# Holding the fourth batch's DMA transposes until half of the last q has landed, and planning with overlapping VectorE and ScalarE instructions

## The chip, the cores and the metric

One core of one Trainium2 chip. The metric is the device time of one execution in microseconds (us). A "span" is the time from the first to the last instruction on the core; it is about 2 us shorter than the device time.

## The reference, cut to what matters

Four batches of eight heads, 768 tokens, 64 columns a head. Attention is local (16 keys on each side) plus one summary key and value per block of 32. Its output feeds eight experts, weighted by a matrix that eight Sinkhorn iterations balance.

```python
def _attn_ref(q, k, v):                     # (4, 8, 768, 64)
    k_sum = k.reshape(B, H, nb, 32, D).max(axis=3)
    v_sum = v.reshape(B, H, nb, 32, D).mean(axis=3)
    # scores with the near keys (masked band) and with the summaries (+ log 32), one softmax over both
    ...
def _moe_ref(x, w_gate, w1, w2):            # x (3072, 512), 8 experts, F = 1024
    P = np.exp(logits - logits.max())
    for _ in range(8):
        P /= P.sum(1, keepdims=True) + 1e-09
        P /= P.sum(0, keepdims=True) + 1e-09
        P *= N / E
    for e in range(E):
        out += P[:, e:e + 1] * (np.maximum(x @ w1[e], 0.0) @ w2[e])
```

## The kernel before

The kernel does not list its instructions in the order in which they are emitted. It describes units of work (engine, estimated cost in us, what they depend on, a priority), and a planner on the host simulates them once and emits the units in the order of that simulation. On the chip each engine then runs its own fixed order and waits where a semaphore isn't set.

```python
class Plan:
    HOP = 0.15
    ...
    def order(self):
        ...
            for u in left:
                t0 = ready(u)
                for e, cost in u.eng.items():
                    t = max([t0, free.get(e, 0.0)]
                            + [d.end + d.lag + (self.HOP if d.on != e else 0.0) for d in u.deps])
                    best.setdefault(e, []).append((t, u, cost))
            ...
            u.start, u.end, u.on = t, end, e
            free[e] = end            # the engine is free when its unit ends
```

A pair of heads is a chain of such units. Pairs 12 to 15 are the fourth batch; their q and k are transposed by DMAs from SyncE's queue, those of the pairs before by TensorE.

```python
# pair_start, pair_whole: the units of one pair, with their planned costs
U["tr", i, z] = add("SP", 1.4, lambda z=z: tr_dma(i, z), [U["kq"[z], i], U.get(("S", i - 3, 1))] + ...)
U["ks", i] = add("DVE", 0.95, lambda: key_max(i), [U["kT", i, 0], ...])
U["km", i] = add("DVE", 0.23, lambda: key_max_split(i), [U["ks", i]] + ...)
U["Vs", i] = add("DVE", 0.28 if i < PB else 0.7, lambda: block_out(i), [U["vs", i], sc], ...)
U["mk", i, h] = add("DVE", 0.56, lambda h=h: masks(i, h), ...)            # twice
U["ed", i] = add("DVE", 0.78, lambda: edges(i), ...)
U["ss", i, 0] = U["ss", i, 1] = add("PE", 0.22, lambda: summaries_2(i), [U["km", i], U["kT", i, 1], ...])
U["sx", i, h] = add("ACT", 0.46, lambda h=h: summary_exp(i, h), [U["ss", i, h]], ...)
U["no", i, h] = add("DVE", 0.75, lambda h=h: normalize(i, h), ...)        # twice
...
rows = add("DVE", 1.65, sink_rows, prev, 0)                               # 8 routing iterations

def edges(i):                      # four small instructions on 32 partitions each
    for j in range(2):
        q0 = 64 + 32 * j           # where the output starts: partition 64, then 96
        nc.vector.tensor_tensor(out=ee[q0:q0 + 32, ...], in0=er[0:32, ...], in1=band[0:32, ...], op=ALU.mult)
        nc.vector.tensor_tensor(out=ee[q0:q0 + 32, ...], in0=er[96:128, ...], in1=band[96:128, ...], op=ALU.mult)
```

TensorE has plenty of work that no pair needs at once (the first expert's products `hps` and `yps` of earlier batches), and the planner fills with it.

The softmax here doesn't subtract the row's maximum and nothing guards it: scores larger than these inputs give would overflow.

## Time and profile before

| | before |
|---|---|
| time, median of 3 runs | 666.03 us (665.86 to 666.69) |
| span of the profiled run | 664.1 us |
| TensorE busy | 656.6 us, 99% |
| VectorE, ScalarE busy | 550.1 us (83%), 410.9 us (62%) |
| TensorE's idle waits after the first 20 us | one, 0.6 us |

What pair 12 does in the kernel before, on VectorE and TensorE (all engines' timeline, start us, length us):

```profile
91.82 0.95 DVE L335 TENSOR_REDUCE ks<-kT 128x24 bf16<-128x768 bf16 x1
...
92.80 0.22 DVE L341 TENSOR_TENSOR ksT<-ks,own 128x64 bf16<-128x64 bf16 x1
...
94.90 0.49 PE L461 MATMUL ss<-qT,ksT 128*128 128x384 bf16 x2
```

The maximum over each block of keys, its split over the two heads, and the scores with the summaries.

### The profile page before, as it was taken

The numbers are of one execution on the slowest core, as the hardware profiler recorded it, in microseconds if no ns is written. First come the engines' busy times: TensorE is split into PE (matmuls) and PEld (weight loads), VectorE is DVE, ScalarE is ACT, GpSimd is POOL, SyncE is SP. The second block draws the span as 40 slices with busy tenths as digits, with TensorE's granted clock in tenths as the row PEclk, the third lists the DMA queues.
The fourth block names the chain that finished last, engine by engine and source line by source line (L and its number), as shares of the span: only waits on it lengthen the run. The fifth ranks groups of instructions, "written<-read, shape, count | busy, mean of one in ns | idle before, by whom it ended". The sixth has DMA issues, their size and how long they took to land.

```text
span 664.1 us, 13257 instructions
## 1 busy us (share of the span) xinstructions
PE 656.6 (99%) x5131; PEld 435.9 (66%) x5132; DVE 550.1 (83%) x1036; ACT 410.9 (62%) x769; POOL 199.0 (30%) x257
## 2 busy tenths in 40 slices
PE   8999999999999999999999999999999999999997
PEld 4666666545766666666666666666666666666666
DVE  7899897799988887887779877988778877988776
ACT  6677676556885566556665665555655656556652
POOL 8899522100132222212322222223122213222123
PEclk9999999999999999999999999999999999999999
DMA  9999932700953747373754665373838465335656
GB/s 167 181 145 145 143 70 43 128 1 2 157 96 65 126 75 118 64 128 65 110 97 71 121 91 101 64 127 65 127 64 135 73 96 96 64 64 112 157 134 202
DMA packets 112558, 67.89 MB, mean 102 GB/s; under 512 B 77936, under 2 KB 90480, under 8 KB 112496
## 3 DMA queue, kind: packets, MB, share of 16 engines
q0 software_dynamic: 94816, 57.46, 64.9%
q1 hardware_dynamic: 17152, 9.58, 5.9%
q8 instruction: 40, 0.66, 0.4%
q14 instruction: 22, 0.18, 0.1%
q10 hardware_dynamic: 528, 0.02, 0.0%
HBM read 52.45 MB, written 6.29 MB: 88 GB/s over the span
## 4 chain that ended last, share of the span: by engine, by line
PE 96%; DVE 3%; DMA 1%; issue 0%; ACT 0%; POOLq 0%; DVEq 0%
PE yps L815 22%; PE pA L764 22%; PE pY L815 17%; PE pQ L764 11%; PE hps L211 6%; PE yps L216 6%; PE pR L764 5%; PE sg L347 1%; DMA qst<-in_q_dram 1%; PE av L512 1%; PE vs L357 1%; PE tkq L303 1%; PE av L435 1%; DVE xs L543 1%; PE ss L461 1%; PE av L441 1%
## 5 line engine op out<-in xcount | busy, mean ns | idle before, releaser
L815 PEld LDWEIGHTS <-h 128*128 128x128 f16 x2352 | 230.1, 98 | 88.5 <-issue 1.0
L843 POOL DMA_DIRECT2D out_acc<-y x120 | 101.7, 891 | 372.1 <-ACT y L839 110.3
L839 ACT ACTIVATE y<-pY,P_sb 128x256 f32<-128x256 f32 x168 | 79.8, 477 | 123.3 <-PE pY L815 121.6
L830 DVE SCALAR_TENSOR_TENSOR out_acc<-yps,P_sb,out_acc 128x512 f32<-128x512 f32 x128 | 95.1, 744 | 29.0 <-PE yps L815 29.0
L798 DVE TENSOR_TENSOR h<-h 128x1024 f16<-128x1024 f16 x168 | 109.3, 683 | 1.4
L815 PE MATMUL pY<-w,h 128*128 128x256 f16 x672 | 100.0, 273 | 0.6 <-ACT y L839 0.6
L815 PE MATMUL yps<-w2sum,h 128*128 128x256 f16 x672 | 98.4, 273 | 0.0
L764 PE MATMUL pA<-xT,w 128*128 128x512 f16 x336 | 98.3, 379 | 0.0
L815 PE MATMUL yps<-w,h 128*128 128x256 f16 x672 | 93.3, 273 | 0.0
L830 DVE SCALAR_TENSOR_TENSOR out_acc<-pY,P_sb,out_acc 128x512 f32<-128x512 f32 x84 | 62.8, 748 | 29.1 <-PE pY L815 27.4
L764 PEld LDWEIGHTS <-w 128*128 128x128 f16 x672 | 65.8, 98 | 31.6 <-issue 0.2
L764 PEld LDWEIGHTS <-w1sum 128*128 128x128 f16 x504 | 49.3, 98 | 45.0
L786 DVE CUSTOM_DVE_ANT_0 h<-pQ,snap 128x512 f16<-128x512 f32 x84 | 57.6, 685 | 7.0 <-ACT snap L207 4.3
L786 DVE CUSTOM_DVE_ANT_0 h<-pA,snap 128x512 f16<-128x512 f32 x84 | 57.3, 682 | 4.8 <-PE pA L764 4.8
L202 ACT ACTIVATE h<-pA 128x512 f16<-128x512 f32 x84 | 50.6, 603 | 12.6 <-PE pA L764 12.4
L202 ACT ACTIVATE h<-pR 128x512 f16<-128x512 f32 x84 | 50.1, 596 | 8.0 <-PE pR L764 7.7
L207 ACT COPY pR<-pA 128x512 f32<-128x512 f32 x83 | 47.5, 572 | 7.7 <-PE pA L764 6.9
L815 PE MATMUL pY<-w2sum,h 128*128 128x256 f16 x336 | 50.4, 273 | 0.0
L764 PE MATMUL pA<-xsum,w 128*128 128x512 f16 x168 | 50.0, 379 | 0.0
L764 PE MATMUL pR<-xT,w 128*128 128x512 f16 x168 | 50.0, 379 | 0.0
L764 PE MATMUL pQ<-xsum,w1sum 128*128 128x512 f16 x168 | 50.0, 379 | 0.0
L764 PE MATMUL pA<-xsum,w1sum 128*128 128x512 f16 x168 | 50.0, 379 | 0.0
(150 smaller groups left out, 854.3 us busy)
## 6 DMA issues: line engine op xcount, KB each, us to landing
out_acc<-y POOLq DMA_DIRECT2D x120, 256.0 KB, 3.4
w<-in_moe_w_dram POOLq DMA_DIRECT2D x14, 1024.0 KB, 10.7
out_dram<-out_acc SPq DMA_DIRECT2D x24, 256.0 KB, 2.4
qst<-in_q_dram POOLq DMA_DIRECT2D x32, 96.0 KB, 5.3
vx<-in_v_dram POOLq DMA_DIRECT2D x15, 192.0 KB, 6.2
kst<-in_k_dram POOLq DMA_DIRECT2D x24, 96.0 KB, 5.6
w<-in_moe_w_dram POOLq DMA_DIRECT2D x4, 256.0 KB, 7.6
w<-in_moe_w_dram POOLq DMA_DIRECT2D x2, 512.0 KB, 7.7
```

The source lines that it names most:

```text
L202: nc.scalar.activation(out=out, in_=in_, func=AF.Relu, bias=0.0, scale=1.0)
L207: (nc.scalar.copy if eng == "ACT" else nc.vector.tensor_copy)(out=out, in_=in_)
L211: nc.tensor.matmul(hp[:, 0:n], lhsT=w1s[e][:, dk, f * 128:(f + 1) * 128], rhs=xT[:, dk, t0:t0 + n], start=(dk == 0), stop=(dk == KD - 1))
L216: nc.tensor.matmul(yp[:, d], lhsT=h[:, f, c * 128:(c + 1) * 128], rhs=w2s[e][:, f, d], start=(f == 0), stop=(f == KF - 1))
L303: nc.tensor.transpose(t[:, g * 128:(g + 1) * 128], st[:, g, :, :].rearrange("p j d -> p (j d)"), ident)
L764: nc.tensor.matmul(dst[:], lhsT=lhsT, rhs=rhs, start=first and k == 0, stop=k == HK - 1, skip_group_check=True)
L786: nc.vector._custom_dve(dve_ops.TENSOR_ADD_SAT, out=ring(e, p, q)[:, q % 2, blk, :], in0=at[src, e, p, q][:], in1=at.pop(("snap", n, e, p, ...
L798: nc.vector.tensor_tensor(out=h[:, :, out_, :], in0=h[:, :, a, :], in1=h[:, :, b, :], op=op)
L815: nc.tensor.matmul(dst[:, d], lhsT=lhsT, rhs=rhs, start=f == 0 and n in (1, 5, 2), stop=f == HF - 1, skip_group_check=True)
L830: nc.vector.scalar_tensor_tensor(out=o, in0=y, scalar=scalar, in1=o, op0=ALU.mult, op1=ALU.add)
L839: nc.scalar.activation(out=at[key][:, d], in_=src, func=AF.Copy, bias=0.0, scale=P_sb[:, t, e:e + 1])
L843: nc.gpsimd.dma_start(out=o, in_=at.pop(("y", e, p, c, key))[:], accum_op=ALU.add)
```

## The change

It has two intents. The transposes of pair 12, and behind them in SyncE's queue all eight of the batch, are not to mix with the last loads; so GpSimd copies one column of the last q into the targets of pair 12's transposes, which then have to wait for it. And the planner is to know that a VectorE or ScalarE instruction can start before the one ahead has quite ended: after every unit its engine is taken to be free 0.07 or 0.09 us before the unit's end. The routing rows are planned at 1.5 us, not 1.65.

```diff
 class Plan:
     HOP = 0.15
+    OVERLAP = {"DVE": 0.07, "ACT": 0.09}
...
-            free[e] = end
+            free[e] = end - self.OVERLAP.get(e, 0.0)
...
-    X_BY_DMA = 12
-    WHOLE = 10
+    X_BY_DMA = {12, 13, 14}
+    WHOLE = {10, 11, 12, 13, 14, 15}
...
+        def loads_landed(i):
+            st = at["st", NP - 1, 1]
+            for t in (kT[i % NB][0:32, 0:1], qT[i % NB][0:32, W:W + 1]):
+                nc.gpsimd.tensor_copy(out=t, in_=st[0:32, 0, 0, 0:1])
...
             if i >= BY_DMA:
+                hold = U.get(("tr", i - 1, 1))
+                if i == BY_DMA:
+                    hold = add("POOL", 0.3, lambda: loads_landed(i), [last[0], U["q", NP - 1]] + war_k + war_q, prio)
+                    last[0] = hold
                 for z in range(2):
                     U["tr", i, z] = add("SP", 1.4, lambda z=z: tr_dma(i, z),
-                                        [U["kq"[z], i], U.get(("S", i - 3, 1))] + (war_k, war_q)[z], prio)
+                                        [U["kq"[z], i], U.get(("S", i - 3, 1)), hold] + (war_k, war_q)[z], prio)
...
-            load_pair(i, "" if i == PB else "kqv")
+            for n in range(i, NP) if i == BY_DMA else [i] if PB < i < BY_DMA else []:
+                load_pair(n, "kqv")
...
-            rows = add("DVE", 1.65, sink_rows, prev, 0)
+            rows = add("DVE", 1.5, sink_rows, prev, 0)
```

(Left out: the places where a comparison with 10 or 12 becomes a test of membership, with the same members.)

More of the change, by code (lines that the diff above doesn't have):

```diff
@@ L384, in scores @@
             dst = [[sg[:, j, :] for j in range(2)], None]
-            if i >= WHOLE:
+            if i in WHOLE:
                 dst[1] = at["sg", i, 1] = [bank("a", "sg1") for _ in range(2)]
-            score_mms(i, dst, range(G if i >= WHOLE else HG))
+            score_mms(i, dst, range(G if i in WHOLE else HG))
         def scores_1(i):
@@ L948, in pair_whole @@
             deps = [U["kT", i, 0], U["kT", i, 1], U.get(("ed", i - 2))]
-            bufs = [Buffer("s")] + (2 * [None] if i < WHOLE else [Buffer("a"), Buffer("a")])
-            U["S", i, 0] = U["S", i, 1] = add("PE", 0.4 if i < WHOLE else 0.6, lambda: scores(i), deps, prio,
+            bufs = [Buffer("s")] + (2 * [None] if i not in WHOLE else [Buffer("a"), Buffer("a")])
+            U["S", i, 0] = U["S", i, 1] = add("PE", 0.4 if i not in WHOLE else 0.6, lambda: scores(i), deps, prio,
                                               opens=[x for x in bufs if x is not None])
             U["X", i, 0] = add("ACT", 0.97, lambda: score_exp(i, 0), [U["S", i, 0]], prio, uses=bufs[:1])
-            if i < WHOLE:
+            if i not in WHOLE:
                 buf = Buffer("s")
@@ L978, in pair_whole @@
                                     [U["A", i, h], U.get(("x", i - 2))], prio, uses=[buf])
-            if i >= X_BY_DMA and i % PB < PB - 1:
+            if i in X_BY_DMA:
                 U["xt", i] = add("SP", 1.5, lambda: x_dma(i), [U["no", i, 0], U["no", i, 1]], prio)
@@ L1100, in transposed @@
             nc.gpsimd.tensor_copy(out=warm[:, 1:2], in_=qT[r][0:32, W:W + 1])
-            if X_BY_DMA < NP:
+            if NP - 2 in X_BY_DMA:
                 nc.gpsimd.tensor_copy(out=warm[:, 4:5], in_=xT[0:32, PB - 2, (B - 1) * S:(B - 1) * S + 1])
@@ L1108 @@
         last[0] = add("POOL", 0.3, transposed, [last[0], U["near", NP - 1]] + [U["kT", NP - 1, z] for z in range(2)]
-                      + [U["x", i] for i in range(X_BY_DMA, NP - 1)])
+                      + [U["x", i] for i in X_BY_DMA])
         load("w1n", lambda: load_w1(1), 0.85, 5.0)
```

## The prediction

> **What bounds the kernel now.** I read the page's head first, then the chain of work that ended last, TensorE's waits after the start, and only then the stretch that the change touches (60 to 120 us), engine by engine. The page:
>
> ```profile
> span 664.1 us, 13257 instructions
> PE 656.6 (99%) x5131; PEld 435.9 (66%) x5132; DVE 550.1 (83%) x1036; ACT 410.9 (62%) x769; POOL 199.0 (30%) x257
> ...
> PE 96%; DVE 3%; DMA 1%; issue 0%; ACT 0%; POOLq 0%; DVEq 0%
> ```
>
> The reader is to see that TensorE is nearly the whole chain, and that all else on it is 4% of 664.1, some 27 us. A busy TensorE need not be at its rate, so I checked that in the groups of TensorE for 200 to 600 us (names, shape, count, busy us, mean ns):
>
> ```profile
> L815 PE MATMUL pY<-w,h 128*128 128x256 f16 x525 | 78.9, 273 | 0.0
> L764 PE MATMUL pA<-xT,w 128*128 128x512 f16 x264 | 77.7, 379 | 0.0
> ...
> L764 PE MATMUL pQ<-xT,w1sum 128*128 128x512 f16 x132 | 39.3, 379 | 0.0
> ```
>
> All groups of that answer together are 1840 matmuls of 256 columns and 924 of 512. The means, 273 and 379 ns, are latencies: in the chain eight of the first start within 0.87 us (109 ns each) and four of the second within 0.86 us (215 ns each). 1840 x 0.109 + 924 x 0.215 = 200.6 + 198.7 = 399 us of 400. So the 400 us have no hole to win. TensorE's waits from 20 us to the end are a single line:
>
> ```profile
> PE pY L815 <- ACT y L839: 0.6, 1, 0.6
> ```
>
> That one wait is at 657.5 us, in the last tile. In the first 20 us the waits are 1.3 us (zeros), 0.8 us (first q) and 0.3 us (k), all before 7 us. What the schedule could still win is thus about 0.6 us at the end and small switches in the first 30 us.
>
> Now the transposes on SyncE's queue, the scores on TensorE that use them, and GpSimd's loads (start us, length us):
>
> ```profile
> 66.23 1.32 SPq L330 DMA_TRANSPOSE kT<-kst  x1
> 68.01 1.56 SPq L330 DMA_TRANSPOSE qT<-qst  x1
> ...
> 78.48 2.25 SPq L330 DMA_TRANSPOSE kT<-kst  x1
> ...
> 87.99 1.21 SPq L330 DMA_TRANSPOSE qT<-qst  x1
> ```
> ```profile
> 91.06 0.59 PE L347 MATMUL sg<-qT,kT 64*128 64x160 bf16 x12
> ...
> 97.72 0.59 PE L347 MATMUL sg<-qT,kT 64*128 64x160 bf16 x12
> ...
> 103.58 0.59 PE L347 MATMUL sg<-qT,kT 64*128 64x160 bf16 x12
> ...
> 109.26 0.59 PE L347 MATMUL sg<-qT,kT 64*128 64x160 bf16 x12
> ```
> ```profile
> 75.52 0.82 POOL L284 DMA_DIRECT2D qst<-in_q_dram  x1 [0.75 <-DMA kst<-in_k_dram]
> 76.62 1.02 POOL L289 DMA_DIRECT2D vx<-in_v_dram  x1 [0.28 <-DMA qst<-in_q_dram]
> 87.93 0.57 POOL L377 DMA_DIRECT2D Ve<-vx  x1 [10.29 <-PE av L441]
> ```
>
> The last four score groups are pairs 12 to 15 (16 pairs, the fourth batch last). Pair 12's first transpose is issued at 66.23, its scores run at 91.06: 25 us early. The last load of q is issued at 75.52, and GpSimd then idles for 10.29 us.
>
> **What the Trainium skill says.** "DMA: Bandwidth & Descriptors", section "Issuing engines are not separate DMA queues": transfers from all queues end on the same 16 engines and interleave. The trace agrees: the load of half a q takes 5.3 us to land (median of 13) between 40 and 66 us, without transposes, and 7.7 us (of 5) between 66 and 80 us, after the first two. The same page, "Rules for kernel authors", says that a transpose next to ordinary DMAs needs nothing: so the new wait isn't needed for correctness, it only moves traffic; no run here shows more. "Perfetto Trace Analysis", section "Identifying the Most-Contended Engine", calls matmul busy time a bad measure of distance to the roofline; the 273 ns against 109 ns above agree, hence the count of starts. "VectorE: DVE Perf Modes", section "The DRAIN you can't avoid", says that the next operation doesn't start until the pipe is empty. By the trace's recorded ends the starts do overlap: two add-relu of 0.68 us start 0.60 us apart (138.99 and 139.59), while subtractions that read the one before start 0.72 us apart (134.28 and 135.00). The change's 0.07 us fits the first kind.
>
> **The change part by part.**
> 1. The sets for which pairs go by DMA or score whole are written differently, with the same members: 0.
> 2. Loads of pairs 12 to 15 become one block. GpSimd issues them back to back already, one pair in about 4.3 us (k's first halves at 63.07, 67.41, 71.65), in the same order: 0 on the path.
> 3. A new GpSimd step of two tiny copies from the last q into the targets of pair 12's transposes. Similar copies there took 0.17 and 0.21 us: 0.4 us, in the idle 10.29 us. Off the path.
> 4. That step holds SyncE's transposes. Without transposes in flight GpSimd's waits of 0.42 + 0.75 us before the last two q halves (73.95 and 75.52) should go, so the last half is issued near 74.3; plus 5.5 us to land, 79.8; plus copies and semaphores, 80.3. Estimate: pair 12's transposes start 14 us later, near 80.3. On quiet engines one was issued 1.39 us after another (84.48 to 85.87) and landed in 2.7 us. Eight take 11.1 us: the last is issued near 90.0, landed near 93. Both operands of pair 12 have landed by 80.3 + 1.4 + 2.7 = 84.4, or 6.7 us before its scores at 91.06; pair 13 by 87.2 (10.5 us before 97.72); pair 14 by 90.0 (13.6); pair 15 by 92.8 (16.5). A key maximum on VectorE (0.95 us) and its split (0.22 us) fit before the summaries at 94.90. So the whole delay is hidden. Removed: two or three us of slower landing for loads that nobody on the path waits for: 0.
> 5. The planner's overlap (0.07 us VectorE, 0.09 us ScalarE) and 1.5 for 1.65 us alter only the order in which instructions are emitted. No instruction gets shorter and the count of matmuls stays. The real step from one row half of the routing iteration to the next instruction is 1.53 us (124.58 to 126.11), so the new figure is closer. Worth between -0.8 us (the wait of 0.6 at the end and some head switches) and +1 us (a new bubble where VectorE is later than planned); centre -0.2.
> Sum: 666.03 - 0.2 = 665.8 us.
>
> **Rivals.** (a) The hold becomes the path: pair 12's scores wait. For: fixed orders do not wait politely. Against: 6.7 us of slack, and first-layer matmuls of earlier batches fill TensorE there. If the last q lands 10 us late, up to 3 us are lost: 669. (b) VectorE binds in the routing stretch, 121 to 164 us, where it is busy 8.7 to 9.6 of each 10 us. An overlap that dependent steps do not have puts its results later than planned and TensorE waits. Against: TensorE is 100% busy there, a multiply-add that needs the routing result first runs at 169.26, 5 us after it is done at 163.98. Would make 667 to 668. (c) Transposes without rival traffic let the fourth batch and the routing end several us sooner: still nothing, since TensorE has other work throughout; 665.8. (d) The better plan repairs the end and the head: 664.9.
>
> **Range and chances.** (c) changes nothing, (d) takes 0.9, small bubbles of (b) add 1: 8 in 10 between 664.8 and 667.0. Faster by 2% would need 13.3 us, more than all of TensorE's idle time (664.1 - 656.6 = 7.5 us): 0.01. Slower by 2% needs a stall of 13 us, twice pair 12's slack: 0.02. Within 2%: 0.97.
>
> **What would show it.** Right: first transpose near 80 us, the eight steadily about 1.4 us apart, loads of the fourth batch landing in about 5.5 us instead of 7.7; pair 12's scores without a wait for a DMA; TensorE's busy time within 0.5 us of 656.6 and no waits between 20 and 655 us. Wrong: a TensorE wait ended by kT, qT or their DMA near 80 to 110 us (a), or waits ended by VectorE after 121 us (b), or a much changed wait in the first 30 us or the last 6 us (d). A longer span with the same waits would mean a lower granted clock, not this change.

## More of the kernel before

On the page, each digit is the busy share, in tenths, of one fortieth of the span (16.6 us):

```profile
DVE  7899897799988887887779877988778877988776
```

VectorE is the second engine: in the first seven slices, where attention runs, it is busy for 70 to 100% of the time. So a result can come late by standing far back in VectorE's queue.

## The result

| | before | after |
|---|---|---|
| time, median (6 runs each) | 666.25 us (665.86 to 666.69) | 666.88 us (666.82 to 668.52) |
| ratio | | 1.0014, 95% interval 1.0001 to 1.0027 |
| span of the profiled run | 664.1 us | 665.3 us |

A ratio is the mean time of one kernel's runs over that of the other's in the same rounds, so not quite the ratio of the medians. All outputs are right. The change costs 0.6 us by the medians: within 2%, inside the predicted range, and in the other direction than the predicted centre. The times alone show it barely: the interval starts at 1.0001, and that of a second set of runs (after_again, below) is 0.9992 to 1.0018, though both pairs of medians differ by 0.63 us. What carries it is the traces.

The page of the changed kernel:

```profile
span 665.3 us, 13288 instructions
...
PE 657.8 (99%) x5131; PEld 435.9 (66%) x5132; DVE 562.9 (85%) x1051; ACT 403.7 (61%) x754; POOL 199.4 (30%) x259
```

TensorE has the same 5131 matmuls, and 1.2 us more of "busy". (Fifteen instructions went from ScalarE to VectorE, so the planner changed more than the order. That is not what costs the time: true_costs, below, has 1052 on VectorE, 562.4 us busy, and takes the time of the kernel before.) Its waits after 20 us are again a single line, the old one:

```profile
PE pY L822 <- ACT y L846: 0.6, 1, 0.6
```

So by the usual views nothing has happened, and the span is still 1.2 us longer. The hold did what it was meant to do (GpSimd's and SyncE's timelines):

```profile
75.86 0.82 POOL L285 DMA_DIRECT2D qst<-in_q_dram  x1 [0.42 <-issue]
...
80.52 0.18 POOL L338 COPY kT<-qst 32x1 bf16<-32x1 bf16 x1 [2.82 <-ACT out_acc L208]
```
```profile
80.73 1.32 SPq L331 DMA_TRANSPOSE kT<-kst  x1
...
91.19 1.21 SPq L331 DMA_TRANSPOSE qT<-qst  x1
```

The first transpose goes at 80.73 instead of 66.23, the eighth at 91.19, 1.4 to 2.1 us apart; all have landed by 93.92. The routing's first matmul ran at 121.62 (before 123.62) and its last at 156.54 (before 163.09): 6.5 us sooner, for no gain. It is the overlap's order that brings it forward and not the hold: the last one ran at 156.12 without the hold (overlap_only, below) and at 164.97 with the hold but without the overlap (hold_sink).

**Where the time went.** The ends of matmuls are modelled, and a wait of some 0.2 us can vanish inside the modelled tail of the group ahead. It shows only in starts. TensorE's timeline of the changed kernel:

```profile
84.74 0.50 PE L557 MATMUL tx<-ident_x,xs 128*128 128x128 f16 x6
85.07 0.50 PE L364 MATMUL vs<-vx,m_blk 128*128 128x128 bf16 x6
...
89.72 0.50 PE L557 MATMUL tx<-ident_x,xs 128*128 128x128 f16 x6
90.28 0.50 PE L468 MATMUL ss<-qT,ksT 128*128 128x384 bf16 x2
```

The same six transposes of 128 columns, both "0.50 us" long. After the first the next group starts 0.33 us later, after the second 0.56 us later: a wait of 0.23 us for `ksT` that no waits view shows. I did this for the whole trace: for each two consecutive TensorE instructions the step from start to start, less the median step of such a couple (told by the two shapes) over the traced kernels; what is over 0.04 us I call a **short wait**, and I sum those that are not inside one group of the same kind. (The 0.6 us wait of the waits view is one of them, 0.73 us by this measure.)

| short waits, us | before | after |
|---|---|---|
| 20 to 125 us | 0.57 (at 20.6, 43.7, 66.2) | 1.49 (at 20.9, 33.8, 49.4, 53.7, 55.9, 71.6, 72.7, 90.3, 108.9) |
| 125 to 640 us | 0.00 | 0.09 |
| 640 us to the end | 1.02 | 0.90 |

1.49 + 0.09 + 0.90 - 0.57 - 1.02 = 0.89 us. The span without the head (from TensorE's first transpose of q on) grew from 657.10 to 657.93 us, 0.83 us. So these waits are the loss. The other 0.37 us of the 1.2 are in that head, whose loads vary from run to run: a second trace of the changed kernel had 6.87 us there where the first had 7.33, and the same short waits within 0.02 us at the same places.

Why was `ksT` late? VectorE's timeline of the changed kernel:

```profile
84.45 0.55 DVE L419 TENSOR_TENSOR em<-er,band 128x768 bf16<-128x768 bf16 x1
85.02 0.19 DVE L427 TENSOR_TENSOR Ee<-er,band 32x80 bf16<-32x80 bf16 x1
85.22 0.20 DVE L431 TENSOR_TENSOR Ee<-er,band 32x80 bf16<-32x80 bf16 x1
85.43 0.19 DVE L427 TENSOR_TENSOR Ee<-er,band 32x80 bf16<-32x80 bf16 x1
85.63 0.20 DVE L431 TENSOR_TENSOR Ee<-er,band 32x80 bf16<-32x80 bf16 x1
85.86 0.29 DVE L370 TENSOR_TENSOR Ve<-vs,own_n 64x128 bf16<-64x128 f32 x1
...
86.59 0.54 DVE L205 TENSOR_SCALAR h<-hps 128x384 f16<-128x384 f32 x1
87.06 0.94 DVE L342 TENSOR_REDUCE ks<-kT 128x24 bf16<-128x768 bf16 x1
87.92 0.18 DVE L549 RECIPROCAL rc<-av 128x6 f32<-128x6 f32 x1
...
90.02 0.21 DVE L348 TENSOR_TENSOR ksT<-ks,own 128x64 bf16<-128x64 bf16 x1
```

Pair 12's key maximum is done at 88.0, but its split `ksT` stands behind two normalizations and another block copy, and VectorE does these without a gap until 90.02. The transposes are not the reason: that k had landed at 83.6. And the reader sees which instructions overlap: the relu at 86.59 lasts 0.54 us and the next starts 0.47 us after it; the four edge products last 0.19 or 0.20 us and start 0.20 to 0.21 us apart, and the first starts 0.57 us after a mask of 0.55 us. They do not overlap at all.

The Trainium skill, "VectorE: DVE Perf Modes", section "Two Vector instructions with no wait between them", gives a model for it: an instruction is held until all before it have finished when one of its inputs or its output starts in another group of 32 partitions than the last one in the same memory did. The edges read from partition 0 and 96 in turn and write to 64 and 96, so all four should be held; the trace agrees.

Summed for one pair (eight VectorE units: key maximum, split, block copy, two masks, edges, two normalizations): the old plan has 0.95 + 0.23 + 0.70 + 2 x 0.56 + 0.78 + 2 x 0.75 = 5.28 us, the new one 8 x 0.07 less, 4.72 us. The trace's steps give 0.86 + 0.13 + 0.73 + 0.47 + 0.57 + 0.84 + 0.68 + 0.70 = 4.98 us. The old plan was 6% too slow, the new one is 5% too fast.

### The profile page after: what moved, and what is told of

Read it like the earlier page. It is cut to its first block, busy times and chain, and to the rows that moved or that the text cites. A ratio compares the mean times of both kernels' runs of the same rounds, so it can differ in the third digit from the quotient of the medians.

```text
span 665.3 us, 13288 instructions
## 1 busy us (share of the span) xinstructions
PE 657.8 (99%) x5131; PEld 435.9 (66%) x5132; DVE 562.9 (85%) x1051; ACT 403.7 (61%) x754; POOL 199.4 (30%) x259
## 4 chain that ended last, share of the span: by engine, by line
PE 96%; DVE 2%; DMA 1%; issue 0%; ACT 0%; POOLq 0%; DVEq 0%
PE yps L822 22%; PE pA L771 22%; PE pY L822 17%; PE pQ L771 11%; PE yps L217 6%; PE hps L212 6%; PE pR L771 5%; PE sg L354 1%; DMA qst<-in_q_dram 1%; PE tkq L304 1%; PE vs L364 1%; PE av L519 1%; PE av L442 1%; PE ss L468 1%; PE av L448 1%; PE tx L557 1%
## 5 line engine op out<-in xcount | busy, mean ns | idle before, releaser
L822 PE MATMUL yps<-w2sum,h 128*128 128x256 f16 x672 | 100.5, 273 | 0.0
L822 PE MATMUL yps<-w,h 128*128 128x256 f16 x672 | 90.5, 273 | 0.0
L771 PE MATMUL pQ<-xT,w1sum 128*128 128x512 f16 x168 | 50.0, 379 | 0.0
```

The costliest lines, as they stand in the source:

```text
L771: nc.tensor.matmul(dst[:], lhsT=lhsT, rhs=rhs, start=first and k == 0, stop=k == HK - 1, skip_group_check=True)
L822: nc.tensor.matmul(dst[:, d], lhsT=lhsT, rhs=rhs, start=f == 0 and n in (1, 5, 2), stop=f == HF - 1, skip_group_check=True)
```

## The experiments

**Theory 1:** the overlap is taken off units that have none, so the plan is optimistic, and TensorE arrives before VectorE and ScalarE at several places. **Rivals:** the hold costs it; the new figure of the routing rows costs it; or any change of a figure reshuffles the order, and the waits are luck (the lottery). One kernel could not be had: the hold alone, with both old planner figures, does not build, because its order locks up while it is being emitted.

A table at its end collects the short waits and spans (without order_only, late_x2 and late_x4). Each kernel was timed in five rounds against the kernel before on the same chip.

### The parts apart

*overlap_sink*: the change without the hold.

```diff
-                hold = U.get(("tr", i - 1, 1))
-                if i == BY_DMA:
-                    hold = add("POOL", 0.3, lambda: loads_landed(i), ...)
-                    last[0] = hold
-                                        [U["kq"[z], i], U.get(("S", i - 3, 1)), hold] + (war_k, war_q)[z], prio)
+                                        [U["kq"[z], i], U.get(("S", i - 3, 1))] + (war_k, war_q)[z], prio)
-            for n in range(i, NP) if i == BY_DMA else [i] if PB < i < BY_DMA else []:
-                load_pair(n, "kqv")
+            load_pair(i, "" if i == PB else "kqv")
```

> The change without its hold: both planner figures stay (overlap, 1.5 us), loads and transposes as before. First theory (the planner's figures alone reorder TensorE's work and leave six or seven short waits of 0.1 to 0.2 us in the attention stage, about 0.6 us in all): 666.8 to 667.0 us, with short TensorE waits between 40 and 125 us summing to 0.5 us or more, and first transposes near 66 us. Rival (the hold costs the time): 666.2 us. Third (any change of a plan figure throws the order anew, without a sign): anything from 665.7 to 667.2 us.

*overlap_only*: the same, and the routing rows back at 1.65 us.

> Only the overlap of 0.07 and 0.09 us in the planner; routing rows at 1.65 us, no hold. First theory: most of the 0.6 us is here, 666.6 to 667.0 us. Rival (hold): 666.2 us. Third (a new throw): 665.7 to 667.2 us, and not the time of the run with both figures.

*sink_only*: without the hold, without the overlap (`OVERLAP = {}`), rows at 1.5 us.

> Only the routing rows planned at 1.5 instead of 1.65 us. It can alter the order after 118 us alone. First theory and rival: 666.2 us, as the kernel before, with the same TensorE waits before 118 us. Third: 665.9 to 666.6 us.

*hold_sink*: the hold and 1.5 us, `OVERLAP = {}`.

> The hold, the block of loads and 1.5 us, but no overlap in the planner (the hold with both old figures does not build: the order it gives deadlocks). First theory: near before, 666.0 to 666.4 us, with short TensorE waits in the attention stage no larger than before's 0.2 us. Rival (hold costs): 666.8 us or more, with TensorE waits ended by the transposes or what reads them after 80 us. Third: 665.7 to 667.2 us.

Measured: 667.61, 666.83, 666.22 and 666.53 us, where the kernel before had 666.47. The short waits between 20 and 125 us were 1.63 and 1.37 us in the two with the overlap, 0.58 and 0.67 us in the two without. So the overlap is what brings them, and neither the hold nor the rows' figure. Two times missed what I expected: overlap_sink came out 0.6 us above its range, hold_sink 0.1 us. The times alone would not carry this: of the four only overlap_sink's interval (1.0006 to 1.0048) leaves out 1, and one of its runs took 672.01 us.

overlap_sink has a wait that the full change lacks. TensorE's and SyncE's timelines:

```profile
81.07 0.36 PE L442 MATMUL av<-vx,em 128*128 128x65 bf16 x6
81.48 0.52 PE L448 MATMUL av<-Ve,Ee 128*128 128x130 bf16 x3
```
```profile
71.70 1.26 SPq L331 DMA_TRANSPOSE qT<-qst  x1
73.08 0.59 SPq L384 DMA_DIRECT2D Ve<-vx  x1
```

Six products of 65 columns start 0.41 us before the group that needs the copied near values `Ve`; in traces without a wait that step is 0.18 us. Those copies stand behind two transposes in SyncE's queue, were issued at 73.08 to 75.02 and landed at 81.26 to 82.22. In the changed kernel the order puts them ahead of all transposes: issued from 72.11 on, landed by 79.85, no wait there. That is what the hold is worth: some 0.4 us at this place, of which the change then loses a part elsewhere (overlap_sink 1.74 us of short waits up to 640 us, the change 1.58).

### The wait itself

*order_only*: the order of the changed kernel, but GpSimd's two copies go to a scratch corner, so that nothing waits for them at run time.

```diff
-            for t in (kT[i % NB][0:32, 0:1], qT[i % NB][0:32, W:W + 1]):
+            for t in (warm[:, 5:6], warm[:, 6:7]):
                 nc.gpsimd.tensor_copy(out=t, in_=st[0:32, 0, 0, 0:1])
```

> The changed kernel with its whole order (TensorE's is the same, row for row), but the two copies go to a scratch tile, so that nothing waits for the last q: the first transpose starts near 75 us instead of 80.7. If the run-time wait is what the overlap's order needs (the run without the hold showed pair 10's copies of neighbouring values landing at 81.3 to 82.2 us and TensorE waiting 0.39 us for them): those copies land after 81 us again, TensorE waits 0.2 to 0.4 us near 81.5 us, and the time is 0 to 0.4 us above the changed kernel's of the same call. If the wait itself cost the 0.6 us: 666.2 us. The wait of 0.23 us at 90.3 us of the changed kernel should be gone if the late transposes cause it.

*after_again*: the changed kernel unaltered, on the same chip.

> The changed kernel unaltered, to stand beside the others of this call: 666.7 to 667.2 us, with the same short TensorE waits (49, 54, 56, 72, 90, 109 us) in the trace. If these waits are an accident of one profile, they move or vanish.

Measured: 667.03 and 667.05 us (before: 666.42; both intervals include 1). Without the wait the first transpose went at 76.44 instead of about 80.7 (in a trace that is 1.65 us late from 20 us on, where TensorE had waited 1.0 us for weights), the near values landed by 80.77, and TensorE did not wait for them; I had expected 0.2 to 0.4 us there. The other short waits were the change's, one by one, the 0.23 us for `ksT` too: the late transposes don't cause it. So the run-time wait does nothing to the time: the hold acts through the order that it makes the planner choose.

*late_x2* and *late_x4*: how much slack do the held transposes have? Pair 12's transposes are done twice, or four times, one after another.

```diff
-            nc.sync.dma_start_transpose(out=..., in_=...)
+            for _ in range(2 if i == BY_DMA else 1):        # late_x4: 4
+                nc.sync.dma_start_transpose(out=..., in_=...)
```

> The changed kernel with each transpose of pair 12 done twice, one after the other: pair 12's q lands some 6 to 8 us later, near 92 us, still before its scores at 94.4 us. If the whole delay is hidden, as predicted: the changed kernel's time, 666.7 to 667.3 us, no TensorE wait for qT or kT. If the hold already sits on the path: 670 us or more.

> The same with four times: pair 12's q lands near 104 us, after the planned scores at 94.4 us. TensorE's fixed order must stop there: a wait of some 9 to 11 us for qT and a time of 674 to 679 us. If TensorE's other work could still hide it: 667 us.

Measured: 670.36 us (ratio 1.0059, 1.0043 to 1.0076) and 681.34 us (1.0221, 1.0206 to 1.0235), both above what I had expected. In late_x2's trace q landed at 92.55, and the first to wait was not the scores group but the scores with the summaries:

```profile
92.69 0.48 PE L469 MATMUL ss<-qT,ksT 128*128 128x384 bf16 x2 [1.01 <-DMA qT<-qst]
```

In the changed kernel q lands at 85.0 and is wanted from about 90, k lands at 83.6 and is wanted by the key maximum at 87.06: 5 and 3.5 us of slack. Of late_x2's 3.3 us over after_again, 1.4 us are its short waits (2.89 against 1.49 us between 20 and 125 us); its traced run also had 1.5 us more in the first 20 us, at a lower granted clock (0.91) there. The spread of its runs (669.07 to 672.20 us) I cannot explain further. late_x4 brings q 17 us late, and TensorE's waits view has

```profile
PE ss L469 <- DMA qT<-qst: 6.8, 1, 6.8
PE tx L558 <- DVE xs L551: 4.9, 2, 4.7
```

The hold is free because the queue behind it is quick, not because there is no end to the slack.

### How much overlap

*half* (0.035 and 0.045 us), *double* (0.14 and 0.18 us) and *dve_only* (0.07 us for VectorE, none for ScalarE), all with hold and 1.5 us:

```diff
-    OVERLAP = {"DVE": 0.07, "ACT": 0.09}
+    OVERLAP = {"DVE": 0.035, "ACT": 0.045}      # half
+    OVERLAP = {"DVE": 0.14, "ACT": 0.18}        # double
+    OVERLAP = {"DVE": 0.07}                     # dve_only
```

> The changed kernel with half of the planner's overlap (0.035 us for VectorE, 0.045 us for ScalarE); hold and sink figure kept. Theory 1 (the overlap makes the plan optimistic for the units that do not overlap, so TensorE arrives ahead of VectorE and ScalarE and waits a few tenths of a us several times between 20 and 125 us): the short TensorE waits there sum to 0.3 to 0.8 us, between the 0.3 of the kernel without overlap (hold_sink) and the 1.1 of the full change; time about 666.6 to 666.8, +0.1 to +0.4 us on the kernel before. Rival theory 2 (any change of a cost figure deals a new order at random, and the sum of short waits is a lottery without a trend): the sum can be anything from 0.2 to 1.5 us, with no relation to the size of the figure.

> The changed kernel with twice the planner's overlap (0.14 us and 0.18 us), hold and sink figure kept. Theory 1: more optimism, more waits: the short TensorE waits between 20 and 125 us sum to 1.5 to 3 us, and the time is 0.3 to 1.5 us over the full change's, 667.2 to 668.4. Rival theory 2 (lottery): no more than the full change's, 666.3 to 667.0.

> The changed kernel with the overlap for VectorE alone (ScalarE's figure 0), hold and sink figure kept. Theory 1, with VectorE as the engine that most of the short waits name (five of seven): the waits between 20 and 125 us stay at 0.7 us or more and the time within 0.2 us of the changed kernel's. Rival theory 3 (ScalarE's figure makes the bad order: the summary exponential is planned at 0.37 us and takes 0.51): the waits fall under 0.5 us and the time returns to that of the kernel before, 666.2 to 666.5.

Measured: 667.41, 676.11 and 667.41 us (before: 666.24). double went the way of theory 1 and much further than I said: 4.47 us of short waits up to 125 us and 5.76 us after. After the first 20 us, its waits fill eight lines of the waits view, and all but one of the eight name VectorE; three of them:

```profile
PE tx L557 <- DVE xs L550: 0.8, 3, 0.4
...
PE sink L596 <- DVE csum_sb L590: 0.8, 2, 0.4
PE ss L468 <- DVE ksT L348: 0.6, 2, 0.4
```

In the expert stretch it loses about 0.5 us in every expert, at the same four places every 73 us (245.7 and 246.3, 319.1 and 319.7, 392.5 and 393.1, ...): a wrong order in a part that repeats is paid each time. half contradicts theory 1: half the overlap, and 1.74 us of short waits, more than the whole one. dve_only kept the waits (1.98 us), which speaks against ScalarE's figure alone, but was 0.4 us slower than the change, where I had expected 0.2 at most.

### The costs as measured

*true_costs*: overlap and hold stay, and the units that do not overlap, or were planned too short already, get their measured step plus the overlap.

```diff
-            U["ed", i] = add("DVE", 0.78, ...)
+            U["ed", i] = add("DVE", 0.90, ...)
-            U["Vs", i] = add("DVE", 0.28 if i < PB else 0.7, ...)
+            U["Vs", i] = add("DVE", 0.28 if i < PB else 0.79, ...)
-                U["sx", i, h] = add("ACT", 0.46, ...)                       # whole pairs
+                U["sx", i, h] = add("ACT", 0.60, ...)
-                U["kT", i, z] = add({"ACT": 0.8, "DVE": 0.95 if i < PB else 0.56}, ...)
+                U["kT", i, z] = add({"ACT": 0.8, "DVE": 0.95 if i < PB else 0.65}, ...)
-            rows = add("DVE", 1.5, sink_rows, prev, 0)
+            rows = add("DVE", 1.6, sink_rows, prev, 0)
```

> The changed kernel with overlap and hold kept, and the planned cost of those units that the trace shows not to overlap raised to their measured steps: edges 0.90 for 0.78, summary block copy 0.79 for 0.70, summary exponential 0.60 for 0.46, PSUM copies of whole pairs 0.65 for 0.56, routing rows 1.6 for 1.5. Theory 1: VectorE and ScalarE are then planned as they run; the short TensorE waits between 20 and 125 us fall from 1.1 us to 0.4 us or less, and the time falls to 666.0 to 666.4, at or under the kernel before. Rival theory 2 (lottery): waits of 0.6 us or more at other places, time like the changed kernel's.

*edges_cost*: of these only the first two. *true_hop*: true_costs with `HOP = 0.16`, to shuffle the order.

> The changed kernel with overlap and hold, of the corrected costs only VectorE's two: edges 0.90 for 0.78 and the summary block copy 0.79 for 0.70; summary exponential, PSUM copies and routing rows as in the change. Theory 1: most of the short waits of the change named VectorE through the key summaries, whose VectorE queue holds these two units, so the waits between 20 and 125 us fall from 1.49 to 0.5 to 1.0 us. Rival theory 3 (the summary exponential on ScalarE carries the error): they stay at 1.2 us or more.

> The kernel with overlap and the measured unit costs (true_costs), with the planner's semaphore hop at 0.16 instead of 0.15 us, to shuffle the order. Theory 1: true costs keep their low waits whatever the shuffle: 0.7 us or less between 20 and 125 us, time 665.9 to 666.6. Rival theory 2: the low waits of true_costs (0.46 us) were luck; here 1 us or more.

Measured: true_costs 666.33 us (before 666.24), 0.45 us of short waits up to 125 us (0.4 expected at most) and 0.56 us after. edges_cost 667.43 us (before 666.22), 0.97 us: VectorE's two figures remove half of the excess waits there, but another 0.71 us stood after 125 us and the time did not fall. true_hop 666.24 us, 0.46 us: with measured costs the low waits survive a shuffle.

### Luck or optimism

*jitter*: an overlap of 0.005 us on both engines. *pessimist*: the overlap with its sign turned round, so that each engine is planned free later than its unit ends.

```diff
-    OVERLAP = {"DVE": 0.07, "ACT": 0.09}
+    OVERLAP = {"DVE": 0.005, "ACT": 0.005}      # jitter
+    OVERLAP = {"DVE": -0.07, "ACT": -0.09}      # pessimist
```

> The changed kernel with an overlap of 0.005 us on both engines, far too small to be wrong by itself but enough to turn ties in the planner; hold and sink figure kept. Theory 1: like no overlap: short waits between 20 and 125 us of 0.4 to 1.0 us, time 666.2 to 666.8. Rival theory 2 (lottery: the order changes, so the waits change): waits anywhere from 0.3 to 1.8 us; above 1.2 us would show that the order's luck alone is as large as the effect of the full overlap.

> The changed kernel with the overlap's sign turned round: VectorE is planned free 0.07 us later and ScalarE 0.09 us later than their unit ends; hold and sink figure kept. Theory 1 (only optimism costs): TensorE is never planned ahead of VectorE, the short waits between 20 and 125 us stay at 0.7 us or less (the kernel without overlap had 0.67, the full change 1.49, twice the overlap 4.47), time 666.0 to 666.8. Rival theory 2 (lottery, any departure costs): waits of 1.2 us or more as with the full change, time 667 or more.

Measured: jitter 666.45 us with 1.11 us of short waits up to 125 us, pessimist 680.12 us (before 666.22; ratio 1.0222, 1.0190 to 1.0255). Theory 1 in its simple form fell: with slower figures TensorE was to wait for nobody, and it waited 13.3 us in sum. Its longest wait, on TensorE and VectorE:

```profile
187.48 1.40 PE L822 MATMUL pY<-w2sum,h 128*128 128x256 f16 x8 [2.47 <-DVE w2sum L746]
```
```profile
183.01 3.81 DVE L805 TENSOR_TENSOR h<-h 128x1024 f16<-128x1024 f16 x6
186.74 1.41 DVE L746 TENSOR_TENSOR w2sum<-w,w2sum 128x1024 f16<-128x1024 f16 x2
```

VectorE does six sums of `h` before the sum of weights that TensorE stands for. The order has it so. So I read the holes of each plan out of the planner itself: for two consecutive TensorE units, the planned start of the second less the planned end of the first. This is no measurement of the chip; it is what the planner believed.

**Theory 4**, which replaces theory 1: a run's short waits are the holes of its own plan, which an optimistic plan hides and a pessimistic one creates; where the costs are as measured, the run shows the plan's holes and nothing else. Two kernels with true_costs' unit costs were chosen by their plans, before they ran: *measured_overlap*, with the overlap as traces have it, and *planned_hole*, with a hop of 0.17 us, whose plan happens to have 1.87 us of holes up to 125 us.

```diff
# both on top of true_costs
-    OVERLAP = {"DVE": 0.07, "ACT": 0.09}
+    OVERLAP = {"DVE": 0.077, "ACT": 0.1}        # measured_overlap
-    HOP = 0.15
+    HOP = 0.17                                  # planned_hole
```

> The kernel with the measured unit costs (true_costs), and the overlap set to what the trace of the changed kernel shows, 0.077 us for VectorE and 0.10 us for ScalarE. The planner's own order has TensorE holes of 0.42 us between 20 and 125 us (0.38 of them at 21 us) and 0.03 us from there to 640 us. Theory 4 (with costs as measured, TensorE's short waits are the holes of the plan and no more; optimism adds waits to them, pessimism leaves holes in the plan itself): short waits of 0.4 to 0.7 us between 20 and 125 us, under 0.3 us from 125 to 640 us, time 665.6 to 666.3, at or under the kernel before. Rival theory 2 (the order's luck): 1 us or more in sum.

> The kernel with the measured unit costs (true_costs) and a hop of 0.17 us, at which the planner's order itself has TensorE holes of 1.87 us between 20 and 125 us: 0.42 at 21 us and 0.26, 0.34 and 0.82 us between 64 and 67 us. Theory 4: the run shows these holes, at these places: short waits of 1.4 to 2.0 us between 20 and 125 us, most of them between 62 and 68 us; time about 1.1 us over true_costs, 667.0 to 667.8. Rival theory 2 (waits fall where luck puts them): no more than 0.8 us between 62 and 68 us, or waits at other places.

Measured: measured_overlap 665.72 us (five runs, 665.72 to 665.85), planned_hole 667.17 us; before 666.17 us. measured_overlap has 0.57 us of short waits up to 125 us and none from there to 640. planned_hole has 1.92 us for 1.87 planned. The places fit in part: of 1.42 us planned between 64 and 67 us, 0.79 us showed between 63.8 and 65.9 and another 0.42 at 69.8. By the test ("most of them between 62 and 68 us"; the rival: "no more than 0.8 us" there) the places go to the rival, and only the sum to theory 4. TensorE's timeline of planned_hole:

```profile
64.40 0.51 PE L557 MATMUL tx<-ident_x,xs 128*128 128x128 f16 x6
64.94 0.49 PE L304 MATMUL tkq<-ident,qst 128*128 128x128 bf16 x6
65.40 0.50 PE L364 MATMUL vs<-vx,m_blk 128*128 128x128 bf16 x6
65.87 0.74 PE L577 MATMUL lp<-wg_bf,xT 128*128 128x8 f16 x24
```

Three groups of six times 128 columns, and steps of 0.54, 0.46 and 0.47 us instead of 0.33.

All kernels whose order was in question, by short waits (20 to 640 us). Median span: the kernel before has 664.2 us over 51 runs. "Residue" is what the span grew over before, less what the short waits grew:

| kernel | holes planned, us | short waits, us | median span, us | residue, us | ratio to before (95%) |
|---|---|---|---|---|---|
| before | 1.52 | 0.57 | 664.2 | | |
| measured_overlap | 0.45 | 0.57 | 664.0 | -0.2 | 0.9994 (0.9981 to 1.0008) |
| sink_only | 1.93 | 0.91 | 664.5 | 0.0 | 0.9996 (0.9983 to 1.0009) |
| true_hop | 0.96 | 0.93 | 664.55 | 0.0 | 1.0003 (0.9989 to 1.0017) |
| true_costs | 0.86 | 1.01 | 664.6 | 0.0 | 1.0000 (0.9986 to 1.0014) |
| jitter | 1.52 | 1.11 | 664.7 | 0.0 | 1.0002 (0.9990 to 1.0014) |
| overlap_only | 0.41 | 1.37 | 665.1 | 0.1 | 1.0006 (0.9994 to 1.0018) |
| hold_sink | 1.16 | 1.46 | 664.8 | -0.3 | 0.9999 (0.9987 to 1.0011) |
| after | 0.43 | 1.58 | 665.0 | -0.2 | 1.0014 (1.0001 to 1.0027) |
| after_again | 0.43 | 1.58 | 665.2 | 0.0 | 1.0005 (0.9992 to 1.0018) |
| edges_cost | 0.87 | 1.68 | 665.5 | 0.2 | 1.0014 (1.0002 to 1.0026) |
| overlap_sink | 0.39 | 1.74 | 665.9 | 0.5 | 1.0027 (1.0006 to 1.0048) |
| planned_hole | 1.87 | 1.92 | 665.4 | -0.2 | 1.0019 (1.0006 to 1.0031) |
| dve_only | 0.83 | 1.98 | 665.7 | 0.1 | 1.0017 (1.0004 to 1.0029) |
| half | 2.46 | 2.02 | 665.7 | 0.1 | 1.0017 (1.0004 to 1.0029) |
| double | 0.45 | 10.23 | 674.4 | 0.5 | 1.0147 (1.0133 to 1.0160) |
| pessimist | 22.21 | 13.28 | 678.4 | 1.5 | 1.0222 (1.0190 to 1.0255) |

Three readings. First, the short waits account for the time: through the sixteen rows under before, save the two extremes and overlap_sink with its scattered runs, span and waits agree within 0.3 us. Second, plans with the whole overlap or more and uncorrected costs (after, overlap_only, overlap_sink, double) plan 0.4 us of holes and get 1.4 to 10, and the half-corrected ones (edges_cost, dve_only) plan 0.8 to 0.9 and get 1.7 to 2.0; plans without it, or with less (before, sink_only, jitter, half, pessimist), plan more holes than they get; the four with measured costs (true_costs, true_hop, measured_overlap, planned_hole) get what they plan, within 0.15 us. That holds for the sum and not for the places: true_costs planned 0.42 us near 184 us and none near 246, and its trace has 0.13 us at 182.6 and 0.34 us at 245.7 and 246.3. So "the plan's holes and nothing else" is not shown. half was not optimism: its own plan had 2.46 us of holes. Third, the plan of the change promised 1.52 - 0.43 = 1.1 us fewer holes, and the chip gave 1.0 us more. hold_sink does not fit: it planned 1.16 and got 1.46, most of it in two waits for ScalarE after 125 us (0.34 us at 154 and 0.45 us at 554). At 554 ScalarE's `y` had itself waited 1.05 us for a transfer (`out_acc<-y`), so a short cost of ScalarE's need not be to blame there; the wait at 154 stays open.

measured_overlap is the fastest of all kernels run, 1.0 us of span under the change. Against the kernel before its gain isn't shown: the interval includes 1, and the trace of before has the same 0.57 us of short waits.

## Why the prediction was right or wrong

- **TensorE as the bound, no hole in 200 to 600 us:** right. The change's 0.6 us shows in TensorE's starts alone.
- **Steps 1 to 3 (sets, loads as a block, GpSimd's copies):** right. No trace shows a wait for any of them.
- **Step 4, the hold is hidden:** right in its outcome and in nearly all its times: first transpose at 80.73 (predicted 80.3), pair 12's q landed at 85.0 (84.4), the last transpose at 93.9 (93). The 80.3 was partly luck: it was reckoned for the last half of q, issued near 74.3, and that half was issued at 75.86 and landed at 80.85; the copies waited for the half before it. Wrong in the slack. The 6.7 us were counted to pair 12's scores; the first to need k is the key maximum, the first to need q the summaries. late_x2 showed it: the slack is 3.5 and 5 us.
- **Step 5, the planner's order, -0.2 us: this step failed.** It measured +0.6 us by the medians (666.88 - 666.25) and +0.89 us in the traces' short waits. The step named the right danger ("a new bubble where VectorE is later than planned") and then centred the term on the gain. It also took the figures to "alter only the order", while 15 instructions changed engine. Its two arguments fail. One couple of overlapping add-relus was taken for the whole of VectorE, where edges, masks before them and block copies do not overlap. (The section "The DRAIN you can't avoid" that the prediction cites goes on: "A next op that is not held starts earlier", and points to the rule for held ones quoted above. The prediction left that out.) And "the real step ... is 1.53 us, so the new figure is closer" forgot that the overlap is taken off as well: the rows are planned at 1.50 - 0.07 = 1.43 us, about as far under 1.53 (0.10) as 1.65 was over it (0.12). That figure turned out to be worth nothing either way (sink_only).
- **Rival (a):** did not happen. **Rival (b):** its mechanism is the one that happened, but 20 to 125 us in, while the pairs run, and not in the routing stretch, which had no short wait in the changed kernel. **Rival (c):** its outcome came, routing 6.5 us sooner and for nothing, but not by its mechanism: the overlap's order did it, with or without the hold. **Rival (d):** the tail's wait of 0.73 us is unaltered, and the head won nothing.
- **What would show it:** "A longer span with the same waits would mean a lower granted clock" was wrong. The granted clock is 0.999 in both traces and the waits view has the same line; the extra time was in waits too short for that view, which count as busy.

## What to carry to other kernels

A list scheduler's costs are a coupled set: a correction that is right for one kind of instruction and applied to all makes the plan look better and the run worse, so check a new figure against the measured start-to-start step of every unit, and compare the plan's holes with the run's. If the bounding engine shows 99% busy, read its starts, not its ends: ten waits of 0.1 to 0.2 us are invisible in every view of idle time and cost 1 us. Slack is counted to the first consumer on any engine, here a reduction on VectorE, not to the consumer one has in mind.

## What the Trainium skill lacked or had wrong

- "VectorE: DVE Perf Modes", section "Two Vector instructions with no wait between them", says which instructions are held and not how much the others gain. In the changed kernel's trace 588 of the 1051 VectorE instructions start before the recorded end of the one ahead, by 0.077 us in the mean; the four edge products, held by the page's model, start 0.20 to 0.21 us apart at a length of 0.19 to 0.20 us.
- "ScalarE: Activation LUTs" gives one overlap for back-to-back activations, about 93 ns. In the changed kernel's trace 301 ScalarE instructions start before the recorded end of the one ahead, by 0.105 us in the mean, which roughly agrees; but the exponentials of the summaries (64 partitions) start 0.48 to 0.51 us apart at a recorded 0.47 to 0.49 us, without any overlap, and the page has no rule for that.
- "Perfetto Trace Analysis" warns against matmul busy time and does not say that short waits hide in it: TensorE's busy time rose by 1.2 us with the same 5131 matmuls and the same list of waits.
- No page that I found gives the cost of DMA transposes for the ordinary transfers beside them. Issued behind two transposes, the near-value copies took 7.2 to 8.2 us to land (overlap_sink), ahead of all transposes 5.8 to 6.3 us (the change); the last loads took 5.0 to 6.5 us in the change, 7.5 to 9 us in the kernel before.
